# A table of places in place of the list scheduler, in a fused attention and MLP kernel

## The chip, the cores and the metric

The kernel runs on one core of a Trainium2 chip. A core has a matrix engine (TensorE, PE in the profile), two engines for elementwise work (VectorE, DVE, and ScalarE, ACT), a general one (GpSimd, POOL), and SyncE (SP), which here only issues transfers. Each engine executes its own list of instructions strictly in order; between engines, and between an engine and a transfer, semaphores make one wait for another. Transfers (DMA) are issued by SP, ScalarE and POOL from their own queues and run on 16 shared DMA engines. The metric is the device time of one execution in microseconds (us).

## The reference: what is computed

Attention with a window of 128 positions and 4 sink keys over 4 batches, 8 heads, 768 positions of 64 numbers each; the heads laid side by side give x with 768 rows of 512 per batch. Then a LayerNorm, a two-layer MLP (512 to 2048 to 512), and x added to its result.

```python
keep = (pos_k < 4) | ((rel >= 0) & (rel < 128))
a = softmax(where(keep, q @ k.T / 8, -1e9))
x = concat_heads(a @ v)
xn = (x - mean(x)) / sqrt(var(x) + 1e-6) * g_ln
out = x + maximum(xn @ w_ch1, 0) @ w_ch2
```

## The kernel before

**Tiles and chunks.** The 3072 rows are 24 tiles of 128 rows (tile t, six per batch) and 12 chunks of two tiles (chunk c has tiles 2c and 2c+1). For a chunk, q and k are loaded and transposed (`chunk`, L605), v is loaded (`load_v`, L585), the scores are multiplied out, exponentiated on ScalarE and masked (`attend_tile` L724 for chunks 0 and 1, `attend` L777 for the others), and `value` (L844) multiplies with v, divides by the row sums, takes the LayerNorm's mean and variance, centres the tile (L885) and transposes it into xnt. Then `halves` (L927) or `mlp` (L1006) form the first MLP layer and `wino` (L1074), for all chunks but the first two, the second with seven products p1 to p7 (L1109) of matrix sums s1 to s4 (L1092); the products are added up to the result by VectorE (tm at L1123, o at L1130), and stored by SP (L1070, L1154, L1159).

**How data arrives.** The first chunk's q and k come in as f32 halves by SP and ScalarE (L620), are cast to bf16 (L637) and transposed on TensorE. Chunks 1 to 3 come by POOL and are transposed on TensorE too (n4b in the trace is one such load, transposed at L672). From chunk 4 on q and k are loaded by POOL into buffers nat (L687) and transposed by SP's transposing transfers (L569, kq<-nat). The transposes of the centred tiles are PE transposes for the first two chunks and SP transfers (L569, xnt<-xc) from chunk 2 on. The first four rows of v (the sink keys) for the batches 1 to 3 come in sixteen small SP loads (L535, 3 KB each) into one buffer vc, out of which the tables vs1 (VectorE, L539), vs2 and vs3 (POOL) are made; the table vs0 of batch 0 is made at L707.

**What sets the order.** None of this is emitted directly. 1137 calls of `P.op` record a step each: a name, the engines that can do it with a modelled cost, a priority, a function that emits it, and the buffers that it reads and writes. Buffers belong to rings of a fixed number of slots. `Plan.run` (L115) is a list scheduler: it goes forward in a modelled time, and gives each step an engine, a start and a slot in each of its rings, by priorities and modelled costs of work and transfers. The steps are then sorted by start, and one loop emits them; since each engine executes in that order, the sort decides what stands behind what on every engine and in every queue of transfers. Before the loop, up to 24 us of the plan, idle places of TensorE are filled with products on a tile named junk (L1236), whose results nobody reads.

```python
    order = P.run()
    items = [(o.start, o.seq, o) for o in order]
...
    items.sort(key=lambda z: (z[0], z[1]))
...
            if s < 0:
                nc.tensor.matmul(o[:, 0:-s], lhsT=junk[:, 0:128], rhs=junk[:, 0:-s], start=True, stop=True)
            else:
                o.emit(o.eng)
```

Of the kernel before, what the change touches and what calls it, by code (L numbers as in the profile page):

```python
# [13 lines left out]
class Buf:  # L14


    def __init__(self, name, ring=None):
        self.name, self.ring = name, ring
        self.writers, self.users = [], []
        self.slot = None  # L20
        self.left = 0
# [43 lines left out]
class Plan:  # L65


    SEM = 0.035
    TO_PE = 0.11
    PE_DRAIN = 0.18  # L70
    SWITCH = 0.095
    LANES = 8
    SHARED = 36.0
    MIXED = 1e9
    DMA_BUSY = {}

    def __init__(self):
        self.ops = []
        self.rings = {}
# [25 lines left out]
        self.ops.append(o)  # L105
        return o

    def lat(self, src, dst):
        if src.eng == "PE" and src.dma is None:
            return -self.PE_DRAIN if dst == "PE" else self.SEM  # L110
        return self.TO_PE if dst == "PE" else self.SEM

    WINDOW = {"PE": 0.2, "ACT": 0.25, "DVE": 0.25, "POOL": 0.25, "SP": 0.0}

    def run(self):  # L115
        free = {"PE": 0.9, "ACT": 0.75, "DVE": 0.9, "POOL": 1.5, "SP": 0.75}
        lanes = {"POOL": [0.0] * self.LANES, "HW": [0.0] * self.LANES}
        n_dma = {"POOL": 0, "HW": 0}
        dma_free = {"POOL": 0.0, "HW": 0.0, "all": 0.0}
        mode = "n"  # L120
        ready = [o for o in self.ops if o.n_wait == 0]
        order = []
        tensor = sorted((o for o in self.ops if "PE" in o.engs), key=lambda o: (o.prio, o.seq))
        while ready:
            while tensor and tensor[0].start is not None:
                tensor.pop(0)
            head = tensor[0] if tensor else None
            cand = {}
            first = min([o.prio for o in ready for b in o.bufs if b.ring == "pair" and b.slot is None], default=1e9)
            for o in ready:  # L130
                if "PE" in o.engs and o is not head and o.prio >= PAR["strict"]:
                    continue
                need = [b for b in o.bufs if b.ring and b.slot is None]
                ok, avail, took = True, 0.0, {}
                for b in need:
                    used = [u for s in took.values() for u in s.units]
                    ss = [s for s in self.rings[b.ring] if not s.held and not any(u in used for u in s.units)
                          and not (s.lent and o.prio > first)]
                    if not ss:
                        ok = False  # L140
                        break
                    since = max([min(s.free_at for s in ss)] + [min(free[e] for e in o.engs) - 0.3])
                    s = min((s for s in ss if s.free_at <= since), key=lambda s: (s.rank, s.free_at))
                    took[b] = s
                    avail = max(avail, s.free_at)
                if not ok:
                    continue
                best = None
                for e, (occ, lat) in o.engs.items():
                    r = max([free[e], o.nb, avail + (self.TO_PE if e == "PE" else self.SEM)]  # L150
                            + [d.end + self.lat(d, e) for d in o.deps])
                    if e == "PE" and o.mode_in != mode:
                        r = max(r, free[e] + self.SWITCH)
                    if o.dma is not None:
                        q = "POOL" if e == "POOL" else "HW"
                        r = max(r, lanes[q][n_dma[q] % self.LANES])
                    if best is None or r + lat < best[0] - 1e-9:
                        best = (r + lat, e, r)
                cand.setdefault(best[1], []).append((best[2], o, took))
            if not cand:  # L160
                stuck = sorted(ready, key=lambda o: o.prio)[:8]
                raise RuntimeError("plan stuck: " + ", ".join(
                    f"{o.name}[{','.join(b.name for b in o.bufs if b.ring and b.slot is None)}]" for o in stuck))
            e = min(cand, key=lambda e: min(c[0] for c in cand[e]))
            t0 = min(c[0] for c in cand[e])
            st, o, took = min((c for c in cand[e] if c[0] <= t0 + self.WINDOW[e]), key=lambda c: (c[1].prio, c[1].seq))
            for b, s in took.items():
                b.slot = s
                s.take()
            o.eng, o.start = e, st  # L170
            occ, lat = o.engs[e]
            free[e] = st + occ
            if e == "PE":
                mode = o.mode_out
            if o.dma is None:
                o.end = st + lat
            else:
                busy, first, last = o.dma
                q = "POOL" if e == "POOL" else "HW"
                if st < self.MIXED:  # L180
                    at = max(st + occ + first, dma_free[q], dma_free["all"] if st < self.SHARED else 0.0) + busy
                    dma_free[q] = dma_free["all"] = at
                    o.end = at + last
                else:
                    real = self.DMA_BUSY.get(o.dma, busy)
                    other = dma_free["HW" if q == "POOL" else "POOL"] > st + occ + first
                    at = max(st + occ + first, dma_free["all"]) + real
                    dma_free[q] = dma_free["all"] = at
                    o.end = at + last + max(0.0, busy - real) + (PAR["mix"][q == "POOL"] if other else 0.0)
                lanes[q][n_dma[q] % self.LANES] = o.end  # L190
                n_dma[q] += 1
            for b in o.bufs:
                b.left -= 1
                if b.left == 0 and b.ring:
                    b.slot.give(min(u.start for u in b.users), max(u.end for u in b.users))
            ready.remove(o)
            order.append(o)
            for s in o.succ:
                s.n_wait -= 1
                if s.n_wait == 0:  # L200
                    ready.append(s)
        assert len(order) == len(self.ops), "cycle in the plan"
        order.sort(key=lambda o: (o.start, o.seq))
        return order


def pe(us):
    return {"PE": (us, us + Plan.PE_DRAIN)}


def act(n):
# [13 lines left out]
SW = (0.9, 0.7, 0.9)  # L225
# [4 lines left out]
HW_X = (1.0, -0.2, 0.6)  # L230
SW_2 = (0.65, 0.7, 0.9)
HW_T = (0.10, 0.8, 0.8)

Plan.DMA_BUSY = {SW: 1.03, HW_X: 0.55}

LOW, HIGH = 1e-9, 1e9
NEG = -1e30
NEVER = -1e9

PAR = dict(split=(3, 4, 5, 6, 7), gsum=-8.0, guard=183.0, strict=40.0, win=0.4, tr=-8.0, sc=-5.3, sc1=-2.0, av=2.0, trx=9.0, by_dma=4, x_by_dma=2, g_on_w=2, av2=20.0, avi=1.0, behind=5, gtt=9.0, ramp=0.3, vs0=2.6, vpb=12.0,  # L240
           w1p=(0.15, 1.7, 2.05, 2.8), pm=2, w2p=(4.5, 4.51, 4.52, 4.53), by_tile=2, wino=2, vp=(0.0, 0.1, 2.0, 2.1, 4.2, 4.3), ld1=0.05,
# [3 lines left out]
def general(tc, nc, slots, pairs, ones, ident_f, ident, w1, w2, mhalf, g_s, g_r, q, k, v, out, scale):  # L245
# [23 lines left out]
    with tc.For_i(0, B, 1) as b:  # L269
# [5 lines left out]
        for r in range(RB):  # L275
# [23 lines left out]
            for i, t in enumerate(sc):  # L299
# [74 lines left out]
def kernel(  # L374
# [141 lines left out]
    def picks(e):  # L516
        V.memset(pick, 0.0)
        for a in range(2):
# [761 lines left out]
```

## Time and profile before

| what | us |
| --- | --- |
| three runs | 208.88, 208.98, 209.49 |
| median of the runs | 208.98 |
| span of the profiled execution, from first to last instruction | 206.6 |
| TensorE busy | 199.4 (97%) |
| VectorE busy | 179.6 (87%) |
| ScalarE busy | 119.7 (58%) |
| GpSimd busy | 118.7 (57%) |

One execution was profiled; the profile's own time is its span, and the runs measure a little more than the span, for what lies around the first and last instruction. The granted TensorE clock was 1.000 throughout. A line of the trace reads: start in us, duration in us, engine, line of the kernel, operation, what it writes and from what, and a count where neighbours of one kind are drawn together; in brackets stands how long the engine idled before it and what ended that. SPq, POOLq and ACTq are transfers in the queues of these engines; their duration is that of the issue, not of the transfer. A line of a source view has the shortest, median and longest duration in ns, and the first and last start in us. PEld is the loading of weights into TensorE, which runs beside its products.

### The profile page before, as it was taken

What the parts mean: (1) busy time and instruction counts of PE and PEld (TensorE: products, weight loads), DVE (VectorE), ACT (ScalarE), POOL (GpSimd) and SP (SyncE); (2) the same over time, 40 slices, a digit from 0 to 9 for tenths busy, and PEclk for the clock granted to TensorE, in tenths of its full rate; (3) what the DMA queues carried; (4) which work ended last, traced back from release to release, by engine and by line L of the source; (5) the groups of instructions that cost most, each with busy time, mean ns of one, the idle gap of its engine ahead of it and who ended that gap; (6) DMA issues with size and microseconds to landing.
All of it is one profiled execution on the core that took longest, in us unless ns stands there. A gap on an engine that the chain in (4) does not pass through costs nothing.

```text
span 206.6 us, 6790 instructions
## 1 busy us (share of the span) xinstructions
PE 199.4 (97%) x2766; PEld 165.6 (80%) x2766; DVE 179.6 (87%) x437; ACT 119.7 (58%) x187; POOL 118.7 (57%) x170
## 2 busy tenths in 40 slices
PE   6888999999999999999999999999999999999994
PEld 2557996674698897898998988988988988988993
DVE  7589769899599899899989989989989989998693
ACT  3649477839555655666486486485486585560620
POOL 7977475279039029959649949968627229125000
PEclk9999999999999999999999999999999999999999
DMA  5999999999999999999999999899976411210302
GB/s 117 146 195 195 197 181 205 199 158 171 186 200 124 124 191 101 121 174 101 175 152 137 113 159 143 109 171 114 194 117 101 128 33 23 106 32 19 108 27 84
DMA packets 101341, 27.55 MB, mean 133 GB/s; under 512 B 89652, under 2 KB 99128, under 8 KB 101304
## 3 DMA queue, kind: packets, MB, share of 16 engines
q0 software_dynamic: 67712, 13.37, 81.7%
q1 hardware_dynamic: 33304, 13.43, 34.1%
q8 instruction: 22, 0.36, 0.7%
q10 hardware_dynamic: 288, 0.26, 0.4%
q14 instruction: 15, 0.12, 0.2%
HBM read 27.31 MB, written 6.29 MB: 163 GB/s over the span
## 4 chain that ended last, share of the span: by engine, by line
PE 90%; DMA 3%; DVE 3%; POOL 2%; issue 0%; DVEq 0%
PE one L1109 31%; PE one L1027 20%; PE one L958 12%; PE one L1058 7%; PE one L1020 7%; PE pair L854 5%; PE pair L802 4%; DMA n4b<-in_q_dram 3%; PE one L672 1%; PE pair L721 1%; POOL nat L626 1%; PE one L714 1%; DVE xnt L907 1%; DVE kq L595 1%; POOL vn L589 0%; DVE st L874 0%
## 5 line engine op out<-in xcount | busy, mean ns | idle before, releaser
L1027 PE MATMUL one<-xnt,w 128*128 128x256 bf16 x384 | 46.8, 273 | 0.0
L814 ACT ACTIVATE pe<-pair 128x1024 bf16<-128x1024 f32 (+1 forms) x40 | 36.3, 963 | 18.2 <-PE pair L802 18.2
L1037 ACT ACTIVATE hq<-one 128x512 bf16<-128x512 f32 x58 | 33.4, 590 | 17.9 <-PE one L1020 9.4
L1027 PEld LDWEIGHTS <-w 128*128 128x128 bf16 x384 | 36.3, 98 | 4.0
L1109 PEld LDWEIGHTS <-hs 128*128 128x128 bf16 x320 | 31.0, 98 | 4.0
L882 POOL TENSOR_SCALAR st<-st 128x1 f32<-128x1 f32 x24 | 6.4, 266 | 44.4 <-DVE rec L868 27.5
L826 DVE TENSOR_TENSOR pe<-pe,mask 128x1024 bf16<-128x1024 bf16 (+1 forms) x35 | 27.1, 799 | 1.6 <-ACT pe L814 1.4
L969 ACT COPY tz<-one 128x512 f32<-128x512 f32 x24 | 13.9, 585 | 20.6 <-PE one L958 19.2
L1109 PEld LDWEIGHTS <-hq 128*128 128x128 bf16 x240 | 22.2, 98 | 4.1 <-issue 0.5
L589 POOL DMA_DIRECT2D vn<-in_v_dram x24 | 21.9, 922 | 2.2 <-DMA w<-in_moe_w_ch_dram 1.2
L983 ACT ACTIVATE hq<-hq 128x512 bf16<-128x512 bf16 x24 | 15.1, 630 | 13.1 <-DVE hq L980 12.6
L1109 PE MATMUL one<-w,hq 128*128 128x256 bf16 x160 | 19.2, 273 | 0.0
L980 DVE TENSOR_TENSOR hq<-one,tz 128x512 bf16<-128x512 f32 x24 | 16.4, 684 | 1.9 <-PE one L958 1.0
L1130 DVE TENSOR_TENSOR ot<-one,tm 128x256 f32<-128x256 f32 x40 | 15.9, 412 | 2.1 <-PE one L1109 1.8
L1123 DVE TENSOR_TENSOR tm<-one,x 128x256 f32<-128x256 f32 x40 | 16.6, 414 | 1.2 <-PE one L1109 1.1
L870 DVE TENSOR_TENSOR x<-pair,rec 128x512 bf16<-128x512 f32 x24 | 16.6, 691 | 0.8
L874 DVE BATCH_NORM_STATS2 st<-x 128x6 f32<-128x512 bf16 x24 | 16.5, 687 | 0.2
L1020 PE MATMUL one<-xnt,w 128*128 128x128 bf16 x256 | 16.0, 219 | 0.5 <-DVE xnt L907 0.5
L687 POOL DMA_DIRECT2D nat<-in_q_dram x16 | 14.2, 893 | 3.7 <-DMA w<-in_moe_w_ch_dram 3.7
L938 POOL TENSOR_TENSOR xt<-xnt 128x256 bf16<-128x256 bf16 x16 | 12.2, 778 | 7.1 <-DMA xnt<-xc 7.0
L687 POOL DMA_DIRECT2D nat<-in_k_dram x16 | 14.8, 928 | 2.4 <-DMA w<-in_moe_w_ch_dram 2.4
L1020 PEld LDWEIGHTS <-w 128*128 128x128 bf16 x256 | 14.6, 98 | 1.6 <-issue 0.8
(130 smaller groups left out, 387.7 us busy)
## 6 DMA issues: line engine op xcount, KB each, us to landing
out_dram<-ot SPq DMA_DIRECT2D x17, 256.0 KB
w<-in_moe_w_ch_dram POOLq DMA_DIRECT2D x8, 512.0 KB, 12.8
vn<-in_v_dram POOLq DMA_DIRECT2D x24, 128.0 KB, 6.9
nat<-in_k_dram POOLq DMA_DIRECT2D x17, 128.0 KB, 4.6
nat<-in_q_dram POOLq DMA_DIRECT2D x17, 128.0 KB, 4.9
out_dram<-ot SPq DMA_DIRECT2D x14, 128.0 KB
kq<-nat SPq DMA_TRANSPOSE x32
xnt<-xc SPq DMA_TRANSPOSE x20
```

The costliest lines, as they stand in the source:

```text
L589: loads[b * RB + r, "v"] = P.op(f"vld{t}", {"POOL": (0.87, 0.9)}, prio, lambda e: G.dma_start(bv.t[:, :, 0:64], v[b, :, 128 * r:128 * (r + ...
L687: lambda e, nat=nat, ap=ap: G.dma_start(nat.t, ap), writes=[nat], dma=SW if c < 6 else (*SW[:2], PAR["llag"]), after=behind(c, 0 if soon e ...
L814: P.op(f"ex{c}{hp}", {"ACT": act(2 * n)}, d + 0.1 + 0.05 * j, lambda e, pp=pp, pb=pb: nc.scalar.activation(pb.t[:, :, 0:n], pp.t[:, :, 0:n ...
L826: V.tensor_mul(pb.t[:, :, 0:n], pb.t[:, :, 0:n], mm),
L870: P.op(f"x{t}", {"DVE": dve(512)}, d + xo + 0.11, lambda e: V.tensor_tensor(x.t.rearrange("p (a h c) -> p a h c", a=2, c=64), pv()[:, :, : ...
L874: P.op(f"bn{t}", {"DVE": fix(0.60)}, d + xo + 0.12, lambda e: V.bn_stats(st.t[:, 8:14], x.t), reads=[x], writes=[st, mv])
L958: nc.tensor.matmul(b.t[:, 128 * h:128 * h + 128], lhsT=lt[:, kk, 128 * h:128 * h + 128], rhs=rh[:, kk, :], start=first and h == 0 and kk = ...
L1020: nc.tensor.matmul(ph.t[:, 128 * s:128 * s + 128], lhsT=w1[u // 2][:, j, 128 * s:128 * s + 128], rhs=xnt.t[:, j, 128 * (u % 2):128 * (u % ...
L1027: nc.tensor.matmul(ph.t[:, 256 * s:256 * s + 256], lhsT=w1[ht // 4][:, j, 128 * (ht % 4):128 * (ht % 4 + 1)], rhs=xnt.t[:, j, :], start=j ...
L1037: nc.scalar.activation(hg.t[:, u % 4, :], ph.t, AF.Relu)
L1109: nc.tensor.matmul(at(r), lhsT=get(left, g)[:, v, s, :], rhs=rhs, start=first and n == 0, stop=n == 7, skip_group_check=True)
L1123: return P.op(f"tm{name}_{c}", {"DVE": dve(256, 1.14)}, pr - PAR["kp"], lambda e: V.tensor_tensor(tm[name].t, at(r), xs[i].t[:, sl], op=AL ...
```

## The change

`Plan.run` no longer schedules. Two literals give its answer: SCHEDULE has, for each of the 1137 steps in the order in which they were recorded, a letter for the engine (P, A, V, G, S) and a place in hundredths; SLOTS has a digit for each ring buffer, its slot. The scheduler's model (latencies, windows, costs of transfers, `lat`) goes away. What the steps compute, their dependences, the sort and the loop that emits them are as before; 19 lines fewer stand ahead of the kernel's body, so that L1109 becomes L1090.

```diff
-    SEM = 0.035
-    TO_PE = 0.11
...
     def run(self):
-        free = {"PE": 0.9, "ACT": 0.75, "DVE": 0.9, "POOL": 1.5, "SP": 0.75}
-        lanes = {"POOL": [0.0] * self.LANES, "HW": [0.0] * self.LANES}
...
-            st, o, took = min((c for c in cand[e] if c[0] <= t0 + self.WINDOW[e]), key=lambda c: (c[1].prio, c[1].seq))
...
-        order.sort(key=lambda o: (o.start, o.seq))
-        return order
+        engines = dict(P="PE", A="ACT", V="DVE", G="POOL", S="SP")
+        table = SCHEDULE.split()
+        assert len(table) == len(self.ops)
+        for o, entry in zip(self.ops, table):
+            o.eng, o.start = engines[entry[0]], int(entry[1:]) / 100
+            o.end = o.start + o.engs[o.eng][1]
+        for b, n in zip(dict.fromkeys(b for o in self.ops for b in o.bufs if b.ring), "".join(SLOTS.split())):
+            b.slot = self.rings[b.ring][int(n, 36)]
+            for u in b.slot.units:
+                u.lives.append((min(o.start for o in b.users), max(o.end for o in b.users)))
+        return sorted(self.ops, key=lambda o: (o.start, o.seq))
...
+SCHEDULE = """
...
+SLOTS = """
```

The order that results differs as follows.

- TensorE: the same 288 steps and the same 75 changes between kinds of product; the first 29 steps in the same order; 24 fillers instead of 25. Behind that, neighbours change places: chunk 3's first W1 products (L1027) stand ahead of chunk 2's last three W2 products p4, p5 and p3.
- Engine: twelve steps go from ScalarE to VectorE (evacuations, relus, scalings of W1), nine from VectorE to ScalarE, among them the second cast of the first chunk (L637).
- ScalarE: the activation that brings in the table of Exp (L481) stood first and now stands behind chunk 4's work.
- VectorE: vs0 (L707) moves ahead of the second tile's centring and of the copy with gain (L907) into xnt; vs1 (L539) moves from chunk 2 to a place right ahead of chunk 2's result additions (L1130).
- SP: the sixteen loads of v's sink rows stood one after another at the head. Now the order is: g, two loads of the first chunk, the transpose of tile 5, then the sixteen loads in between the transposes of tiles 4, 6 and of chunk 4's q and k and two stores, with the last of the sixteen right ahead of tile 7's transpose.
- SP's last four stores: first the half that is computed last but one, then the other three. Before, two of them stood ahead of it.
- POOL: the loads of later chunks are issued later, closer to their use.

More of the change, by code (lines that the diff above doesn't have):

```diff
@@ L65 @@
 class Plan:
-    SEM = 0.035
-    TO_PE = 0.11
[L70 to L75, printed above, removed]
     def __init__(self):
@@ L106, in op @@
         return o
[L108 to L113, printed above, removed]
-    def run(self):
-        free = {"PE": 0.9, "ACT": 0.75, "DVE": 0.9, "POOL": 1.5, "SP": 0.75}
-        lanes = {"POOL": [0.0] * self.LANES, "HW": [0.0] * self.LANES}
[L118 to L165, printed above, removed]
-            st, o, took = min((c for c in cand[e] if c[0] <= t0 + self.WINDOW[e]), key=lambda c: (c[1].prio, c[1].seq))
[L167 to L202, printed above, removed]
-        order.sort(key=lambda o: (o.start, o.seq))
-        return order
@@ L207, in pe @@
+PE_DRAIN = 0.18
 def pe(us):
-    return {"PE": (us, us + Plan.PE_DRAIN)}
+    return {"PE": (us, us + PE_DRAIN)}
 def act(n):
@@ L232 @@
 HW_T = (0.10, 0.8, 0.8)
-Plan.DMA_BUSY = {SW: 1.03, HW_X: 0.55}
 LOW, HIGH = 1e-9, 1e9
@@ new lines @@
+V1202 P1181 A1248 G777 G939 P1308 V1533 P1340 A1391 V1615 P1481 A1532 V1742 P1379 A1483 P1858 P1879 V1949 V1973 V2045
+V2118 G2209 V2305 P2355 V2398 P1511 A1624 V1801 P1670 A1765 V1871 P2024 P2045 V2127 V2151 V2223 V2296 G4004 V2458
+P2552 V2633 G1176 G1248 P2671 A2738 P2717 A2830 G1869 G2122 P2956 A3145 V3704 A3053 V3159 A3036 P3381 A3534 V3644
+A3443 V3548 P3785 P3854 V3935 V3959 V4069 V4194 G4216 V4369 S4851 P3806 V3924 V4236 V4309 V4395 G4416 V4568 S4606
+G2892 G2644 P4303 A4417 P4257 A4325 V5066 G3576 G3824 P4541 A4600 V4763 A4670 V4846 P4770 A4899 V4984 A4829 V4926
@@ new lines @@
+P5124 V5197 V5221 V5294 V5393 G5415 V5738 S5816 P5076 V5561 V5585 V5678 V5764 G5785 V5983 S6022 G3482 S4971 G4088
+S5516 G3389 S5091 G3917 S5366 G3141 G2505 P6028 A6139 V6545 A6230 V6452 A6564 P6368 A6581 V6701 A6472 V6641 P6774
+P6843 V6973 V6997 V7117 V7190 G7211 V7316 S7362 P6795 V6902 V7057 V7235 V7307 G7329 V7420 S7482 G6216 S6779 G4508
+S6899 G5868 S6427 G6042 S6557 G6390 G5498 P7599 A7787 G7893 A7678 V7890 A7770 P8026 A8176 V8408 A8085 V8341 P8390
+P8500 V8570 V8617 V8689 V8814 G8836 V9058 S9103 P8593 V8677 V8904 V8976 V9049 G9070 V9312 S9357 G7412 S8325 G6303
@@ new lines @@
+S8085 G7673 S8205 G6129 S8664 V9901 G6477 G5955 P9221 A9279 V9550 A9350 V9434 P9452 A9510 V9693 A9581 V9780 P9938
+V9984 V10008 V10169 V10321 G10342 V10458 S10504 P9962 V10309 V10333 V10491 V10564 G10585 V10706 S10751 G8356 S9752
+G7586 S9872 G8657 S9512 G8197 S9632 G7499 G8110 P10592 A10799 G11016 A10707 V11013 A11082 P10932 A10990 V11211 A11099
+V11286 P11251 P11452 V11658 V11682 V11871 V11943 G12035 V12127 S12226 P11404 V11509 V11533 V11742 V11931 G11952 V12044
+S12106 G10755 S11350 G9872 S11230 G9785 S11110 G10190 S10990 G10103 G10668 P12126 A12315 G12421 A12223 V12818 A12206
@@ new lines @@
+V16721 G16742 V17045 S17090 P16072 V16230 V16254 V16444 V16516 G16538 V16653 S16698 G13725 S15763 G14888 S15608 G14975
+S16073 G15145 S15953 G13812 G16621 P16657 A16736 G16842 A16828 V17284 A17147 P16997 A17055 V17188 A17164 V17344 P17315
+P17469 V17538 V17562 V17699 V17819 G17840 V18139 S18373 P17517 V17622 V17759 V17831 V17956 G17978 V18172 S18218 V3854
+V4892 V4694 V6301 V3315 V4627 V4661 V5354 V3393 V4203 V5527 V6009 V4019 V4594 V5890 V5645 P1550 A1716 P1762 A2085
+P1927 A2036 P2093 A2425 P2180 A2289 P2267 A2376 P2377 A2486 P2465 V2573 P3198 P3428 P3902 P3988 V4129 S4786 P3514
@@ new lines @@
+P4075 P4161 P4359 V4467 S5301 P2574 V2693 P2860 V2968 P2772 V2881 P3285 A3393 P3024 V3219 P3111 A3237 P3688 A3809
+P3601 A3858 P4588 P4674 P4817 P4903 V5096 S6677 P4445 P4990 P5148 P5235 V5402 S7019 V5161 V3888 A5031 A3748 A4970
+V4532 V4727 V3608 V5030 A3626 V3279 A3687 A5654 V4810 A3907 A5092 P5408 A5517 P5321 V5467 P5496 A5604 P5583 A5715
+P5670 V5923 P5932 A6040 P5757 A5866 P5844 A6090 V6109 V6076 V6043 V6153 V6232 V6199 V6797 V6512 P6096 V6265 P6271
+V6380 P6184 V6416 P6415 V6605 P6590 V6761 P6677 V6866 V6830 P6891 V7199 S8784 S8819 P6502 A6673 P7066 A7175 P6979
@@ new lines @@
+A7088 P7153 A7262 P7415 A7524 P7328 A7436 P7240 A7349 P7502 V7611 V7349 V7704 V7671 V7811 V7737 V7857 V8099 V8022
+P7666 V7775 P7754 V7950 P7841 V7986 P7929 V8063 P8073 V8198 P8160 V8269 V8305 P8292 V8581 S9992 S8629 S9477 V5800
+V6913 V8138 V7453 G8038 G8443 G8284 G8585 P8248 A8314 P8455 A8522 P8411 V8477 A8892 P8548 A8614 P8641 V8749 A8843
+P8773 V8839 A8991 P9079 A9150 P8904 A9040 P8817 A8942 P8685 A8794 P8992 A9100 V9243 V9103 V9345 V9164 V9391 V9209
+V9643 V9481 P9124 V9276 P9267 V9829 P9355 V9514 P9498 V9608 P9586 V9744 P9674 V9865 V9931 P9806 V10068 S11505 S10624
@@ new lines @@
+A19117 P19165 V19247 A19324 P19210 V19312 A19389 P19429 A19500 P19254 V19377 P19078 V19187 P18946 V19055 P19342 A19450
+V19593 V19449 V19626 V19514 V19695 V19559 V19794 V19899 P19474 V19659 P19561 V19827 P19649 V19758 P19749 V19863 P19836
+V19945 P19924 V20069 V20033 P20011 V20120 S20152 S20187 S20117 S20222 V18049 P18357 V18511 P20176
+"""
+SLOTS = """
+0001000123001000000301112011130112230130410122211150603331022145102781109010444255503311601012103416603077120345121005
+6210071088209936170134102890101210aa41bb522435056103410051c0020d116307101100671101210e223f3320345231038921003100540445
```

35 lines of the change are left out of this document (added).

## The prediction

> **What bounds the kernel now.** I read the page's first lines first, then the chain of waits, then the busy time by stage.
>
> ```profile
> span 206.6 us, 6790 instructions
> PE 199.4 (97%) x2766; PEld 165.6 (80%) x2766; DVE 179.6 (87%) x437; ACT 119.7 (58%) x187; POOL 118.7 (57%) x170
> PE 90%; DMA 3%; DVE 3%; POOL 2%; issue 0%; DVEq 0%
> ```
>
> TensorE is busy for 97% of the span and holds 90% of the chain that ended last. DVE is the next fullest with 87%, and it is second in nothing that the chain shows. What matters is therefore where TensorE idles at all. The next lines are stages in us: length, busy time of each engine with its count, then granted clock (1.00), DMA share, GB/s.
>
> ```profile
> 13.00:20.00 7.00, 6.27 (x135) 5.03 (x130) 6.45 (x12) 5.84 (x9) 5.26 (x9) 1.00 1.41 199
> 20.00:45.00 25.00, 24.98 (x420) 19.58 (x419) 20.80 (x48) 15.16 (x23) 14.01 (x20) 1.00 1.71 189
> 45.00:60.00 15.00, 15.00 (x158) 9.80 (x154) 12.69 (x32) 10.12 (x16) 7.13 (x11) 1.00 2.08 179
> 60.00:75.00 15.00, 15.00 (x208) 12.74 (x206) 13.55 (x33) 8.28 (x13) 6.94 (x10) 1.00 1.60 145
> 150.00:180.00 30.00, 30.00 (x463) 26.43 (x462) 28.12 (x64) 19.19 (x32) 12.15 (x19) 1.00 0.34 85
> 180.00:203.50 23.50, 23.41 (x252) 20.62 (x249) 19.79 (x50) 8.58 (x16) 4.86 (x8) 1.00 0.16 48
> ```
>
> From 20 us on nothing is idle but 0.02 + 0.09. So 0.73 (13 to 20 us) + 0.11 is all that a better order can win in these rows; a little more hides inside "busy", where a product waits for an operand but its record is drawn long. In the last W2 group the starts tell it:
>
> ```profile
> 185.67 1.05 PE L1109 MATMUL one<-n4a,hs 128*128 128x256 bf16 x8
> 186.67 1.03 PE L1109 MATMUL one<-n4c,hs 128*128 128x256 bf16 x8
> 187.67 0.60 PE L1109 MATMUL one<-w2t,hq 128*128 128x256 bf16 x4
> 67.79 1.05 PE L1109 MATMUL one<-n4b,hs 128*128 128x256 bf16 x8
> 68.67 1.04 PE L1109 MATMUL one<-w,hs 128*128 128x256 bf16 x8
> 69.55 1.91 PE L1027 MATMUL one<-xnt,w 128*128 128x256 bf16 x16
> ```
>
> Eight products that are fed go by in 0.88 (67.79 to 68.67); at 185.67 and 186.67 a step takes 1.00, so 0.25 is lost there. With some 0.2 for others of that kind, the gain can be at most 0.73 + 0.11 + 0.25 + 0.2 = 1.3 us. A loss has no such limit, so the question is which of the moved steps comes too late for TensorE.
>
> **The change part by part.** The 1137 steps, what each depends on and what it computes stay. The order on each engine, the engine of 21 steps and the buffer of each result change. TensorE has the same 288 steps with the same 75 changes of kind, the first 29 in the same order, so its own work costs the same.
>
> *The ramp.* ScalarE's table load (L481) moves from its first place to far behind, so the load now happens before the first thing that ScalarE computes, the cast at L637, whose queue place is behind its waits for the raw loads. The second cast, done by VectorE before, follows on ScalarE.
>
> ```profile
> 1.95 1.28 ACT L481 ACT_TABLE_LOAD   x1 [1.95 <-PEq L1261]
> 5.04 0.62 ACT L637 CAST hq<-n4a 128x512 bf16<-128x512 f32 x1 [1.59 <-DMA n4a<-in_q_dram]
> 12.17 1.02 ACT L758 ACTIVATE pe<-pair 128x1024 bf16<-128x1024 f32 x1 [1.98 <-PE pair L754]
> 12.73 1.08 PE L672 MATMUL one<-ident,n4b 128*64 128x128 bf16 x32 [0.60 <-DMA n4b<-in_q_dram]
> 13.41 1.23 DVE L595 COPY kq<-one 128x1024 bf16<-128x1024 bf16 x1 [0.42 <-PE one L672]
> 18.01 0.69 DVE L907 TENSOR_TENSOR xnt<-one,gt 128x512 bf16<-128x512 bf16 x1
> 18.75 1.05 PE L1020 MATMUL one<-xnt,w 128*128 128x128 bf16 x16 [0.45 <-DVE xnt L907]
> 19.21 0.42 DVE L707 TENSOR_TENSOR vs<-one,sel 128x260 bf16<-128x260 f32 x1
> q0 software_dynamic: 4398, 1.09, 161.1%
> q1 hardware_dynamic: 182, 0.04, 4.3%
> ```
>
> The attention of the first tile is pushed back by about 1.28 + 0.5 (the second cast's wait), taken as 1.6 to 1.8. It has cover: TensorE waited 0.60 for n4b and ScalarE idled 1.98 before its first activation of the second tile; I take 1.3 as hidden and 0.3 as left. The path that releases the solid part is VectorE's run from 13.41 to 18.70; it starts with n4b, which the casts don't touch. Into this run goes L707 with 0.42, behind it before: some 0.3 more. Together +0.6. At the most nothing covers: 1.7 + 0.3 = +2.0. At the least all of it is covered and the small loads of V that leave this stretch hasten n4b: in 5.5 to 12.6 us they are 4.3 beside 161.1, 2.6% of 7.1 us, −0.2.
>
> The Trainium skill ("ScalarE: Activation LUTs", section "What ACT_TABLE_LOAD costs") puts the load at about 1283 ns and adds some 1380 ns of drain on a switch. The row agrees with the first, 1.28 us; the drain isn't seen here, since nothing ran ahead of this load. By the page, an estimate, the sum would be 1.4 us higher.
>
> *The middle.* Sixteen small loads of V (L535) stood at the head of SP's queue; now they stand between the transposes of chunks 2 to 5. Between tile 5's transpose and tile 7's, SP issues seven transposes, all sixteen small loads and two stores. A queue executes in order.
>
> ```profile
> L569 SPq DMA_TRANSPOSE kq<-nat x32: 1190/1220/2368, 53.2 to 159.5; - x32
> L535 SPq DMA_DIRECT2D vc<-in_v_dram x16: 250/298/309, 3.6 to 11.4; - x16
> 57.25 0.53 SPq L1070 DMA_DIRECT2D out_dram<-ot  x1
> 57.88 2.37 SPq L569 DMA_TRANSPOSE kq<-nat  x1
> 62.79 1.19 SPq L569 DMA_TRANSPOSE xnt<-xc  x1
> 94.41 2.00 SPq L569 DMA_TRANSPOSE xnt<-xc  x1
> 100.34 1.29 POOL L938 TENSOR_TENSOR xt<-xnt 128x256 bf16<-128x256 bf16 x2 [1.64 <-DMA xnt<-xc]
> 184.55 1.19 SPq L569 DMA_TRANSPOSE xnt<-xc  x1
> 187.13 1.48 POOL L938 TENSOR_TENSOR xt<-xnt 128x256 bf16<-128x256 bf16 x2 [3.06 <-DMA xnt<-xc]
> 46.24 0.41 DVE L885 TENSOR_SCALAR xc<-x,st 128x512 bf16<-128x512 bf16 x1
> 64.35 0.41 DVE L1130 TENSOR_TENSOR ot<-one,tm 128x256 f32<-128x256 f32 x1
> ```
>
> A transpose holds SP 1.22 us, a store 0.53, a small load 0.30 of its own and (11.4 − 3.6)/15 = 0.52 from start to start: I take 0.40. That is 8.5 + 6.4 + 1.1 = 16.0 us (14.4 with 0.30, 17.6 with 0.5). A transpose right behind a store took 2.37, 1.15 more: one such gives 17.1, which I take, two with the upper price 19.8. The start is the end of tile 5's centring, 46.65, with two 0.4 us VectorE steps now ahead of it and the ramp's 0.6: 48.0. So tile 7's transpose (62.79 before) is issued at 65.1, between 62.4 and 67.8. From issue to use I find 2.6 us (184.55 to 187.13) and 5.9 (94.41 to 100.34); between them 4.25: landed at 69.35. Chunk 3's products (69.55 before) are due earlier, since three W2 groups of 0.87 now come behind them: 69.55 + 0.6 − 2.6 = 67.5. TensorE waits 1.9 us. The ends are 0 (issue by 62.4 and 2.6 of transit) and 67.8 + 5.9 − 67.5 = 6.2.
>
> The vs sums (L539) need all sixteen small loads and stand in VectorE's queue right ahead of the W2 additions that begin at 64.35 (L1130); behind them wait more additions, the masks, and in turn the banks into which TensorE writes. With VectorE at 13.55 of 15.00, a wait here isn't made up soon. I take none of it above the 1.9, because both end with the same run of SP.
>
> *The last groups.* The sums that the products at 185.67 and 186.67 take stand two places earlier on VectorE: −0.25, from 0 to −0.5 with the other small losses.
>
> ```profile
> 202.91 0.96 DVE L1130 TENSOR_TENSOR ot<-one,tm 128x256 f32<-128x256 f32 x2
> 203.35 0.88 SPq L1154 DMA_DIRECT2D out_dram<-ot  x2
> 97.80 0.34 SPq L1154 DMA_DIRECT2D out_dram<-ot  x1
> ```
>
> *The tail.* Before, two of the four last stores went out ahead, and the last was issued at 203.35 + 0.88 − 0.34 = 203.9 (a store of this line holds SP 0.34). Now the store that needs the last addition but one (ready at 203.36) stands first, and three follow at about 0.37 each (0.34 and a gap of 0.03): 204.5. That is +0.6; 1.1 if four stores that leave together also land later by half a step each, 0.5 at the least.
>
> *Costed at nothing.* The large POOL loads come later in POOL's order and nearer to their use. They land ahead of need by the plan's order; what hides them is that a load of 128 KB takes 4.9 us to land, and its transpose sits in an SP queue which is late anyway; without that cover scores of chunks 4 to 5 wait as long as SP does. Twelve steps go to VectorE and nine to ScalarE, so VectorE has three more, at the 0.4 to 0.7 us of its rows above some 2 us in 206.6, spread over stages that have 1.45 to 2.31 free of 15; if all of it fell where VectorE is full, the 2 us would count.
>
> ```profile
> nat<-in_q_dram POOLq DMA_DIRECT2D x17, 128.0 KB, 4.9
> ```
>
> *The sum.* 206.6 + 0.6 + 1.9 − 0.25 + 0.6 = 209.45 us of span. The median of the runs, 208.98, lies 2.38 above the span of the profiled execution; what lies around it is the same: 211.8 us.
>
> **The rivals.**
>
> *SP keeps up.* The queue takes its 14.4 us, transit is 2.6, and the middle costs nothing. For it: the small loads take 0.30, and the transposes rarely wait. Against it: SP starts late, and a store stands in the list. Point: landing of tile 7 before 67.5. Then 211.8 − 1.9 = 209.9.
>
> *VectorE is held as well.* The last small load is issued just ahead of tile 7's transpose, about 64.6, and lands 2.6 to 5.9 later, 67.2 to 70.5, where the additions are due at 65.0: 2.2 to 5.5 us, in which TensorE runs out of banks. The middle, 3.85, is 1.9 more than the forecast's wait: 213.7.
>
> *Faster.* The queue is hidden, the tail's later issue is hidden under the landing of the others, the ramp's idle time and the small steps are won: 208.98 − 1.3 = 207.7, up to 208.3 if half comes. For it: only 0.84 of idle is visible at all, and the small loads leave the busiest stretch of DMA. Against it: the new waits above. Point: the first large W1 group starts before 18.75 and the middle shows no wait.
>
> *No effect.* TensorE is full, so order on the others is hidden both ways: 209.0.
>
> **How the numbers follow.** Forecast 211.8 (from 210.4 to 213.3) 0.43; VectorE held as well 0.12; SP keeps up 0.13; no effect 0.13; faster 0.19. Changes under 0.3%, 0.63 us, can't be told from none, so "same" is 208.35 to 209.6. Faster 0.19, same 0.13, slower 0.68. The range goes from 208.0, which leaves out half of "faster", to 214.2, which leaves out half of "VectorE held": 0.16 outside.
>
> **What would show it.** Ramp: a table load near 4.5 to 6 us and the W1 products that began at 18.75 begin near 19.35. Middle: TensorE idle before chunk 3's first 128x256 products by about 1.9 us, released by the DMA of xnt; the vs sum of L539 after 60 us with a wait for the DMA of vc. Tail: the last store issued about 1.1 us after the last addition began its second half, not 0.5. I am wrong if TensorE shows no idle between 60 and 75 us, or if the first large products start before 18.75.

## The result, and the profile after

The changed kernel takes 223.19 us (median of 4 runs, 222.50 to 225.16) against 209.18 us before: 1.069 times as long (95% interval 1.064 to 1.075). The forecast was 211.8 us, with a range that ended at 214.2. The direction and the two costly places (the middle and the tail) were right; the sizes were not. A few executions take over 1.5% longer than the fastest of the same kernel, and they are left out where they would decide a comparison.

The profiled execution has a span of 221.0 us, 14.4 more than before. The page's first lines and the stages of it (us: length, busy time of TensorE, weight loads, VectorE, ScalarE, GpSimd, then granted clock, DMA share, GB/s):

```profile
span 221.0 us, 6744 instructions
PE 203.1 (92%) x2765; PEld 165.7 (75%) x2765; DVE 178.5 (81%) x440; ACT 117.1 (53%) x184; POOL 115.6 (52%) x170
...
45.00:60.00 15.00, 14.63 (x145) 9.19 (x146) 13.31 (x36) 8.56 (x13) 4.21 (x8) 1.00 1.09 103
60.00:75.00 15.00, 8.93 (x121) 6.98 (x120) 8.55 (x24) 6.33 (x11) 8.56 (x10) 0.95 1.70 140
75.00:90.00 15.00, 15.00 (x180) 12.59 (x179) 11.71 (x29) 6.30 (x10) 5.94 (x9) 0.94 0.78 108
90.00:105.00 15.00, 14.47 (x204) 12.25 (x202) 14.44 (x31) 8.63 (x15) 10.43 (x15) 1.00 1.25 133
105.00:120.00 15.00, 14.37 (x202) 12.33 (x200) 14.17 (x33) 8.26 (x16) 8.36 (x13) 1.00 1.10 115
```

VectorE does no more than before (178.5 against 179.6 us). TensorE lost 6.07 us of 15 between 60 and 75, where it had been full, and its clock was granted at 0.95 from 60 to 75 us and at 0.94 from 75 to 90. The instructions of that place, from the trace of the changed kernel (start, duration, and in brackets the idle time before it):

```profile
64.97 1.19 SPq L550 DMA_TRANSPOSE xnt<-xc  x1
66.20 0.82 SPq L516 DMA_DIRECT2D vc<-in_v_dram  x2
67.12 1.32 SPq L550 DMA_TRANSPOSE xnt<-xc  x1
...
67.72 1.05 PE L1090 MATMUL one<-n4c,hs 128*128 128x256 bf16 x8
...
72.10 0.43 DVE L520 TENSOR_TENSOR vs<-vc,sel 128x260 bf16<-128x260 f32 x1 [5.73 <-DMA vc<-in_v_dram]
...
74.28 1.87 PE L1008 MATMUL one<-xnt,w 128*128 128x256 bf16 x8 [5.51 <-DMA xnt<-xc]
75.94 1.52 PE L1090 MATMUL one<-w2t,hq 128*128 128x256 bf16 x8
77.30 1.04 PE L1090 MATMUL one<-n4b,hs 128*128 128x256 bf16 x8
```

Tile 7's transpose was issued by SP at 67.12; TensorE stood still for 5.51 us until it had landed, and VectorE for 5.73 us until the last small load of V had. The eight products at 74.28 then took until 75.94, 1.66 us where before 0.87 was enough, the next eight 1.36. Short windows over the same place show the clock at that time (columns as above):

```profile
70.00:74.00 4.00, 0.00 (x0) 0.00 (x0) 1.90 (x5) 0.00 (x0) 0.00 (x0) 0.94 2.09 162
74.00:76.00 2.00, 1.72 (x9) 1.26 (x10) 2.00 (x5) 0.00 (x0) 0.00 (x0) 0.50 1.65 172
76.00:78.00 2.00, 2.00 (x16) 1.63 (x15) 0.77 (x3) 0.60 (x1) 0.00 (x0) 0.77 1.23 254
78.00:80.00 2.00, 2.00 (x45) 1.62 (x43) 1.83 (x6) 0.00 (x0) 0.00 (x0) 1.00 0.30 116
```

After the pause the granted clock was 0.50, and 1.00 again only by 78 us. The Trainium skill says why in "TensorE: Matmul & The Clock Gate", section "What's actually happening": after about 3.4 us of idling the clock is gated to half, and it takes as long of work to free it. The trace agrees with the order of size only: if the clock is either whole or half, the shares above put it at half from about 73.5 to 76.9 us (an estimate), that is from 4.7 us into the pause until 2.6 us of work were done.

At the end of the trace of the changed kernel:

```profile
213.72 0.49 PE L1090 MATMUL one<-w,hs 128*128 128x256 bf16 x3
...
214.26 0.96 DVE L1111 TENSOR_TENSOR ot<-one,tm 128x256 f32<-128x256 f32 x2
214.70 1.80 SPq L1135 DMA_DIRECT2D out_dram<-ot  x4
```

TensorE's last group of eight starts 11.35 us later than before (202.37 to 213.72); the other 3.05 us of the 14.4 come behind it. Four stores now leave together from 214.70; the last is issued about 216.1 (214.70 + 1.80 less the 0.4 that an issue takes), and the end comes 4.9 us after that, where before it came 2.7 after (203.9 to 206.6).

The start of the same TensorE step in both traces divides the rest. Before, the second tile's W1 products start at 18.75, and chunk 5's scores and the last group so:

```profile
77.92 0.25 PE L802 MATMUL pair<-kq,kq 64*64 64x64 bf16 x4
202.37 1.04 PE L1109 MATMUL one<-w,hs 128*128 128x256 bf16 x8
```

In the changed kernel the first two are:

```profile
19.00 1.05 PE L1001 MATMUL one<-xnt,w 128*128 128x128 bf16 x16
86.55 0.25 PE L783 MATMUL pair<-kq,kq 64*64 64x64 bf16 x4
```

The W1 products are 0.25 later. Chunk 5's scores are 8.63 later, so 8.4 of it arise between: the wait of 5.51, 1.3 for the half clock, and 1.6 of smaller losses (one is a wait of 0.55 for a transpose of chunk 4's q and k). The last group is 11.35 later, so 2.7 more arise after chunk 5's scores, among others in the stages from 90 to 120 us above, where TensorE is 0.53 and 0.63 short.

### The profile page after: what moved, and what is told of

The parts are those of the page before. It is cut to its first block, busy times and chain, and to the rows that moved or that the text cites. A ratio compares the mean times of both kernels' runs of the same rounds, so it can differ in the third digit from the quotient of the medians.

```text
span 221.0 us, 6744 instructions
## 1 busy us (share of the span) xinstructions
PE 203.1 (92%) x2765; PEld 165.7 (75%) x2765; DVE 178.5 (81%) x440; ACT 117.1 (53%) x184; POOL 115.6 (52%) x170
## 5 line engine op out<-in xcount | busy, mean ns | idle before, releaser
L1008 PEld LDWEIGHTS <-w 128*128 128x128 bf16 x384 | 37.0, 99 | 10.1 <-issue 5.8
L1018 ACT ACTIVATE hq<-one 128x512 bf16<-128x512 f32 x53 | 30.7, 595 | 26.3 <-PE one L1008 16.5
L795 ACT ACTIVATE pe<-pair 128x1024 bf16<-128x1024 f32 (+1 forms) x40 | 36.9, 963 | 12.5 <-PE pair L783 12.5
L1090 PEld LDWEIGHTS <-hs 128*128 128x128 bf16 x320 | 30.2, 98 | 6.0 <-issue 1.7
L807 DVE TENSOR_TENSOR pe<-pe,mask 128x1024 bf16<-128x1024 bf16 (+1 forms) x35 | 24.3, 711 | 2.5 <-ACT pe L795 2.4
L1090 PEld LDWEIGHTS <-hq 128*128 128x128 bf16 x240 | 22.9, 99 | 3.9 <-issue 0.3
L1090 PE MATMUL one<-w,hq 128*128 128x256 bf16 x160 | 19.7, 273 | 0.0
L1073 DVE TENSOR_TENSOR hs<-hq 128x512 bf16<-128x512 bf16 x40 | 15.4, 419 | 2.4 <-ACT hq L1018 2.2
L939 PEld LDWEIGHTS <-hq 128*128 128x128 bf16 x256 | 15.7, 98 | 0.9 <-issue 0.3
L668 POOL DMA_DIRECT2D nat<-in_q_dram x16 | 14.7, 923 | 1.8 <-DMA w<-in_moe_w_ch_dram 1.6
```

Of the source, the lines that this page charges most:

```text
L795: P.op(f"ex{c}{hp}", {"ACT": act(2 * n)}, d + 0.1 + 0.05 * j, lambda e, pp=pp, pb=pb: nc.scalar.activation(pb.t[:, :, 0:n], pp.t[:, :, 0:n ...
L807: V.tensor_mul(pb.t[:, :, 0:n], pb.t[:, :, 0:n], mm),
L939: nc.tensor.matmul(b.t[:, 128 * h:128 * h + 128], lhsT=lt[:, kk, 128 * h:128 * h + 128], rhs=rh[:, kk, :], start=first and h == 0 and kk = ...
L1008: nc.tensor.matmul(ph.t[:, 256 * s:256 * s + 256], lhsT=w1[ht // 4][:, j, 128 * (ht % 4):128 * (ht % 4 + 1)], rhs=xnt.t[:, j, :], start=j ...
L1018: nc.scalar.activation(hg.t[:, u % 4, :], ph.t, AF.Relu)
L1090: nc.tensor.matmul(at(r), lhsT=get(left, g)[:, v, s, :], rhs=rhs, start=first and n == 0, stop=n == 7, skip_group_check=True)
```

## The experiments

S is the theory that the sixteen small loads in SP's queue are the cause; P, that GpSimd's later loads are, by crowding the transfers. In what is expected, theories of one experiment are marked by a letter too (V, D, W, O, X). Where the edit is in the changed kernel, a dictionary of names gives steps another place in the table:

```diff
-            o.eng, o.start = engines[entry[0]], int(entry[1:]) / 100
+            o.eng, o.start = engines[entry[0]], MOVED.get(o.name, int(entry[1:]) / 100)
```

**The small loads back at the head of SP's queue.**

```diff
+MOVED = {f"vcd{i // 4}{i % 4}": 30 + 0.3 * i for i in range(16)}
```

> The changed kernel, but the sixteen small loads of V go back to the head of SP's queue. Theory S (they delay tile 7's transpose and vs1): SP had no gap from 48.8 to 67.1 us, and sixteen loads at 0.30 to 0.47 are 6 us of it, so tile 7's transpose is issued near 61, TensorE's wait of 5.5 us and the slower clock after it (1.1 us) go, and so do VectorE's wait of 5.7 and what came of it later (2.6 us of lag between 90 and 126 us): 223.2 - 9.2 = 214, or 216.6 if the later lag stays. Rival P (POOL issues its loads for chunks 4 and 5 between 62 and 69 us, and they make the transpose's transfer take 7.0 us): the wait stays at 3 us or more, 220 or above.

216.06 us (1.035 of before, 1.027 to 1.042; the changed kernel 1.069). The stage of this run that had the pause, the issue of both chunk 3 transposes, chunk 5's scores and the last group:

```profile
60.00:75.00 15.00, 15.00 (x208) 12.75 (x206) 14.11 (x36) 7.58 (x13) 8.93 (x12) 1.00 1.78 150
```

```profile
59.69 3.12 SPq L550 DMA_TRANSPOSE xnt<-xc  x2
67.14 1.04 PE L1008 MATMUL one<-xnt,w 128*128 128x256 bf16 x8
...
78.14 0.25 PE L783 MATMUL pair<-kq,kq 64*64 64x64 bf16 x4
...
205.31 1.04 PE L1090 MATMUL one<-w,hs 128*128 128x256 bf16 x8
```

TensorE has no gap and a clock of 1.00; chunk 3's products start at 67.14. S holds, P alone does not: GpSimd issues the same eight loads here, about 1 us earlier (61.06 to 68.22). By the medians 7.1 us came back. In the trace all of the middle's 8.4 did: chunk 5's scores are 0.22 later than before. The profiled execution is the fastest of the five (214.40 us); the other four took 215.86 to 216.52 at granted clocks of 0.991 to 0.996, and what they lost is not known. From chunk 5's scores to the last group 127.17 us pass, as in the changed kernel (before 124.45), so the later lag of 2.7 us is not what VectorE's wait leaves behind.

**vs1 six steps later on VectorE, the small loads still between.** `MOVED = dict(vs1=67.3)`

> The changed kernel, but VectorE makes vs1 six steps later, behind the first additions and the masks of chunk 4; the small loads stay between the transposes. Theory S with the transpose as what ends last: TensorE's wait for xnt stays at about 5.5 us, and only what VectorE lost comes back, up to 2.6 us: 220.6 to 223. Rival V (VectorE's wait at vs1 holds up TensorE): the wait shrinks to 2 us or less, 217 to 219.

222.31 us (1.062, 1.054 to 1.071). VectorE's wait is down to 0.93 us, TensorE's is 5.18 (lines of this run):

```profile
71.40 0.43 DVE L520 TENSOR_TENSOR vs<-vc,sel 128x260 bf16<-128x260 f32 x1 [0.93 <-DMA vc<-in_v_dram]
73.24 1.86 PE L1008 MATMUL one<-xnt,w 128*128 128x256 bf16 x8 [5.18 <-DMA xnt<-xc]
```

In the changed kernel it is the transpose that ends last, not VectorE; the difference of 0.9 us between the medians is within the noise. (In the next run, which changes nothing in the middle, the profile puts TensorE's wait of 5.89 us down to a mask of VectorE, L807. In the changed kernel the same product began 0.46 us before that mask had ended, so it doesn't need the mask.)

**The last four stores in the order of before, alone and with the small loads.** `MOVED = dict(st220=200.9, st232=201.0)`; in the second run both sets of places.

> The changed kernel, but the last four stores in the order of before (two of them ahead of the one that needs the last addition but one). If the four stores that leave together are what the tail lost (from TensorE's last product to the end 5.7 us, before 2.7): 223.2 - 3.1 = 220.1. If it is the later issue alone, as the prediction had it: 223.2 - 0.6 = 222.6.

> The changed kernel with both: the small loads at the head and the stores in the order of before. The two are far apart in time, so the gains should add: 214 - 3.1 = 210.9 by theory S, 217 by rival P.

220.79 us (1.055, 1.047 to 1.064) and 212.05 us (1.016, 1.008 to 1.023). By the medians the stores are worth 2.4 us alone and 4.0 beside the small loads. The traces agree on 3.1 in both: from TensorE's last group to the end 4.2 us pass with the old order of the stores (215.30 to 219.5 and 205.67 to 209.9) and 7.3 with the new one. Together the two moves give back 11.1 of the 14.0 us.

**The same two moves alone, in the kernel before.** The scheduler's own places, with a few replaced after it has run:

```diff
-        assert len(order) == len(self.ops), "cycle in the plan"
+        for o in order: o.start = MOVED.get(o.name, o.start)
...
+MOVED = dict(vcd12=48.04, vcd10=48.05, vcd21=50.4, vcd32=53.0, vcd30=53.01, vcd02=53.02, vcd22=54.4, vcd31=57.0, vcd33=57.01, vcd13=57.02, vcd00=57.03, vcd23=57.04, vcd01=57.05, vcd11=57.06, vcd03=58.0, vcd20=58.01, vs1=61.87)
```

> The kernel before, list scheduler and all, but the sixteen small loads of V stand between SP's transposes as in the changed kernel, and vs1 ahead of chunk 2's first result addition. Theory S (these loads alone hold up tile 7's transpose): about 13 of them at 0.45 us come after SP's one long gap, tile 7's transpose is issued near 68 in place of 62.8, TensorE waits 3 to 5.5 us before chunk 3's products: 209 + 3 to 6.5, so 212 to 215.5. Rival P (late POOL loads are needed too, and this kernel's are early): under 1 us, 209 to 210.

219.41 us (1.046, 1.039 to 1.054): more than expected. Lines and stages of this run (the line without a time is of the view of transfers: the time from issue to landing of tile 6's transpose, issued at 65.33):

```profile
xnt<-xc SPq DMA_TRANSPOSE x1, 6.4
68.25 1.19 SPq L569 DMA_TRANSPOSE xnt<-xc  x1
72.45 0.43 DVE L539 TENSOR_TENSOR vs<-vc,sel 128x260 bf16<-128x260 f32 x1 [7.91 <-DMA vc<-in_v_dram]
74.53 1.86 PE L1109 MATMUL one<-w2t,hq 128*128 128x256 bf16 x8 [7.91 <-DVE tm L1123]
```

```profile
60.00:75.00 15.00, 7.09 (x89) 5.82 (x87) 6.59 (x18) 4.25 (x7) 6.50 (x8) 0.82 1.41 141
75.00:90.00 15.00, 15.00 (x187) 11.86 (x186) 11.50 (x28) 7.42 (x11) 3.22 (x6) 0.84 0.17 50
```

The move is enough by itself. Here, with TensorE's old order, VectorE ends last: TensorE waits 7.91 us for an addition queued behind vs1, and works at 0.82 and 0.84 of its clock around that. If the clock is either whole or half, it was at half from about 69.6 to 79.8 us (an estimate from the two shares), 5.3 us of it work, which costs some 2.6 us.

Rival P doesn't get its test here, though: GpSimd's loads are not early in the kernel before either. These are its six of that time:

```profile
62.27 1.87 POOL L687 DMA_DIRECT2D nat<-in_k_dram  x2
64.12 1.78 POOL L687 DMA_DIRECT2D nat<-in_q_dram  x2
65.86 1.79 POOL L589 DMA_DIRECT2D vn<-in_v_dram  x2
```

They leave from 62.27 to 67.65 us (in this run 0.1 later), where the changed kernel issues eight from 62.07 to 69.2. Before, tile 7's transpose was issued at 62.79, when only the first of them had left; in this run tile 6's, at 65.33, comes among them, and it took 6.4 us to land.

For the stores, `MOVED = dict(st220=200.7, st232=200.8)`:

> The kernel before, but of its last four stores the one that needs the last addition but one stands first in SP's queue. If four stores that leave together land late (the run with the stores put back gained 2.4 us): 209 + 2 to 3 = 211 to 212. If only the issue is later, as the prediction had it: 209.6.

211.84 us (1.013, 1.009 to 1.018), span 209.8 us. The stores that leave together cost this kernel 3 us, not 0.6; from its last group to the end 7.3 us pass (202.49 to 209.8).

**Five of GpSimd's late loads later still.** `MOVED = dict(kld61=73.4, qld61=73.5, vld10=73.6, vld13=73.7, vld12=73.8)`

> The changed kernel, with five of the eight loads that POOL issues between 62 and 69 us put behind tile 9's statistics, so that they leave after 84 us. If those loads are why tile 7's transpose took 7.0 us from issue to landing, it lands in about 4.5 and TensorE's wait falls from 5.5 to 3: 220 to 221, if nothing later waits for the five loads. If the transpose is slow for what SP itself issues, the 7.0 and the 5.5 stay: 223 or above.

219.63 and 220.74 us in the two of its four runs that can be compared, near the expected 220 to 221 and below all runs of the changed kernel (222.50 or more); two runs are too few for an interval. The trace, of the run at 220.74, shows the part in question:

```profile
67.10 2.20 SPq L550 DMA_TRANSPOSE xnt<-xc  x1
70.54 0.10 PEld L1008 LDWEIGHTS <-w 128*128 128x128 bf16 x1 [1.14 <-DMA xnt<-xc]
71.12 1.03 PE L1008 MATMUL one<-xnt,w 128*128 128x256 bf16 x8 [1.43 <-DVE ot L1111]
```

Issued at the same 67.1, the transpose is in use 3.4 us later and not 7.2. What TensorE then still waits for is VectorE's addition behind vs1 (ot): in the changed kernel this addition ended at 72.87, so without the late transpose TensorE would have stood there until about 72.9 in place of 74.28 (an estimate). GpSimd's queue between 64 and 74 us (packets, MB, and the time of its packets as a share of the 16 engines' time, which can pass 100%), in the changed kernel and then in this run:

```profile
q0 software_dynamic: 7437, 0.94, 160.1%
```

```profile
q0 software_dynamic: 2909, 0.37, 57.5%
```

So loads that are in flight beside it lengthen the transfer. Chunk 5's scores start at 82.56, 4.0 us earlier than in the changed kernel; then TensorE waits 1.38 us (93.72) and 1.49 us (102.01), the second for a transpose of q and k, and at the last group (211.78) 1.9 of the 4.0 are left.

**ScalarE's table load back at the start**, on top of the run at 212.05 us: `tab0=1.75, tab=1.81`.

> The changed kernel with the small loads at the head and the stores in the old order (212.05 us), and ScalarE's table load back at its first place. In the run without this the load stood at 4.97 us ahead of the first cast, the first tile was 1.6 us behind, and at TensorE's wait for n4b all of it but 0.06 was gone. So by the reading that the wait for n4b covers it: 211.8 to 212.3, the first products of the second tile still near 12.8. By the prediction's +0.3: 211.7.

212.24 us (1.014, 1.006 to 1.022). Where the load stands is not to be seen in the time. TensorE's transposes of n4b start at 12.72 us with the load at the start and at 12.80 without, the second tile's W1 products at 18.87 and 18.89.

**The last 3.3 us.** The run at 212.05 us has a span of 209.9, 3.3 more than before. All of these start from it. First, single VectorE steps (`wsum2=82.9, o4_2=96.91, o4_0=96.92, kts2=99.35, mk71=110.95`), since TensorE's waits there have lines like these of that run:

```profile
84.54 1.15 DVE L904 TENSOR_TENSOR hq<-w,w 128x1024 bf16<-128x1024 bf16 x1
...
85.61 0.74 DVE L1111 TENSOR_TENSOR ot<-one,tm 128x256 f32<-128x256 f32 x2
86.08 1.03 PE L1090 MATMUL one<-w,hs 128*128 128x256 bf16 x8 [0.40 <-DVE ot L1111]
```

> The changed kernel with the small loads at the head and the stores in the old order (212.05 us), and in addition VectorE's additions for chunks 3 to 5 ahead of longer steps (wsum2, two masks, kts2) that stood before them. Theory D (the rest of the loss, about 3.3 us, is TensorE waiting some 0.2 to 0.6 us at a time for a bank that an addition has not freed): five of these waits, 2.0 us together, shrink to 0.5: 210 to 210.7. Rival (VectorE is as full in either order, a wait only moves): 211.7 to 212.3.

211.93 us: nothing. The waits moved: in this run TensorE stands 0.9 us for a mask. Then ten steps back on ScalarE, alone and with these moves:

```diff
-            o.eng, o.start = engines[entry[0]], MOVED.get(o.name, int(entry[1:]) / 100)
+            o.eng, o.start = "ACT" if o.name in ON_ACT else engines[entry[0]], MOVED.get(o.name, int(entry[1:]) / 100)
+ON_ACT = "rl0_7 rl1_0 rl1_1 rl2_1 rl2_4 rl3_7 w1g13 w1g20 w1g22 w1g31".split()
```

> As the run at 212.05 us (small loads at the head, stores in the old order), with the ten relus and scalings of W1 after 20 us that the table moved to VectorE put back on ScalarE at the same places. Theory W (VectorE has 5.1 us of these more and 2.4 us of others less, is 2.3 us behind when chunk 5's scores are multiplied, and TensorE pays in small waits): VectorE comes level, the waits between 85 and 120 us shrink from 2.9 to 1 or less: 209.7 to 210.5. Rival (the order alone, whichever engine): 211.5 to 212.3.

> The same with the additions ahead of wsum2, two masks and kts2 as well. Theory W: with VectorE no longer behind, the order of these steps can count or not, 209.3 to 210.3. Rival: as without it, 211.5 or more. A version of the changed kernel that is faster than the kernel before (208.7) would show here.

212.05 and 212.14 us: nothing either, though VectorE's busy time falls from 178.5 to 173.8. Then VectorE's list in the order of before (130 and 308 places are given anew), and TensorE's with it:

> As the run at 212.05 us (small loads at the head, stores in the old order); VectorE's 150 steps between the places 60 and 128 stand in the order that they had before, every other engine's order is the changed one. Theory O (the last 3.3 us lie in the order of VectorE's list, in many places of it, so that five moves and five microseconds of relief could only shift the waits): the waits between 85 and 120 us go, 2.9 of them, and 209 to 210 us are left. Theory X (the orders of the engines fit each other: VectorE's old order beside the others' new one is no better): 211.5 or more.

> The same, with all of VectorE's steps from place 26 on in the order of before. Theory O: 208.5 to 209.7, since the waits of 20 to 45 us and at 163 us (1.1 together) go too. Theory X: 211.5 or more.

> As the run at 212.05 us, with VectorE's and TensorE's steps from place 60 on in the order of before; ScalarE, GpSimd and SP keep the changed one. Theory O: as the first, 208.5 to 210. Theory X with VectorE and TensorE as the pair that has to fit: 208.5 to 210 here alone, and 211.5 or more in the other two. If GpSimd's late loads and sums hold the rest: 211 or more here as well.

219.29, 237.69 and 221.47 us (medians of the runs that can be compared), all slower. TensorE's longest waits in the second of them (total, times, longest):

```profile
PE one L1090 <- DVE hs L1073: 7.5, 4, 4.0
PE pair L835 <- DVE pe L807: 5.6, 9, 1.2
```

Theory O falls: the old order of one engine, or of two, beside the new order of the others is much worse than either whole. Last, two more steps by hand, wsum2 into a gap (`wsum2=77.5`) and kts2 behind an addition (`kts2=100.7`):

> The changed kernel with the small loads at the head, the stores in the old order, ten relus and scalings back on ScalarE and the five moves (212.14 us), and two more from its trace: wsum2 goes into a gap of 1.15 us in which VectorE waited for the first W2 product of chunk 3, and kts2 behind chunk 4's last addition. If the rest is many small misfits that can be taken out one at a time, 0.9 and 0.6 us of TensorE's waits go: 210.7. If a wait only moves to the next step on the list, 211.7 to 212.3. No version from the table is then expected under 208.9.

211.42 us (1.015, 1.009 to 1.020), the same as 212.14 within its interval. No version made from the table came under the kernel before.

## Why the prediction was right or wrong, point by point

**What bounds.** Right. TensorE had no idle time to give, and the losses that were traced are stretches in which a moved step came too late for it. "At most 1.3 us to win, no limit on a loss" stands.

**Which step failed.** Most of the 11.4 us between the forecast and the result lies in the middle: +1.9 in the sum, +8.4 measured. The wait was 5.51 and not 1.9, and the half clock behind it (1.3) was no term. The next two are the last groups and the orders (−0.25 in the sum, +2.7 measured) and the tail (+0.6 in the sum, +3.05 measured).

**The ramp, +0.6.** The mechanism was right, the size too large: +0.25. The table load did come ahead of the cast (at 5.24 us), and the wait for n4b covered all of it but 0.02 (18.87 and 18.89 with the load at the start and without), where I had left 0.3.

**The middle, +1.9.** The right queue, the right transpose, the right steps; the wait was 5.51. Three numbers of the sum were off. The list was issued from 48.8 to 67.1, 18.3 us in place of 17.1 and 0.8 later: +2.0. The issues by themselves took 17.2, as priced; the other 1.1 are the gaps between them, for which the sum has no term. From issue to use the transpose took 7.2 us, where I had taken the middle between rows of 2.6 and 5.9: +2.9. That row of 5.9 was no upper bound: at 65 to 67 us the transpose comes among GpSimd's loads. In the kernel before they leave from 62.27 to 67.65, so the trace of before already had them at the time that I forecast for the issue, 65.1. That the products were due at 68.77 and not 67.5 took 1.3 off again. The wait lay inside my bounds of 0 to 6.2; a third of the way up was the wrong choice.

**What the pause costs besides, not in the sum.** The half clock: 1.66 + 1.36 in place of 0.87 + 0.88 for two groups, 1.3 us. No row of before shows a pause of that length, and a forecast of 1.9 us gave no reason to look for it; the upper end of 6.2 did.

**VectorE held as well.** It was a rival at +1.9 us. VectorE did wait 5.73 us. Taking that wait away left 5.18 us of TensorE's, because the transpose ends last; with the transpose early (the run with five loads later) VectorE ended last, and so it did in the kernel before with the small loads moved. Two waits at one place do not add up, and here the smaller one stands only some 1.4 us behind the larger.

**The last groups, −0.25.** The mechanism came, the gain did not. The group that starts at 183.90 before, and the same group after:

```profile
183.90 1.91 PE L1109 MATMUL one<-w,hq 128*128 128x256 bf16 x16
```

```profile
195.46 1.91 PE L1090 MATMUL one<-w,hq 128*128 128x256 bf16 x16
197.42 1.05 PE L1090 MATMUL one<-n4a,hs 128*128 128x256 bf16 x8
198.31 1.04 PE L1090 MATMUL one<-n4c,hs 128*128 128x256 bf16 x8
199.18 1.04 PE L1090 MATMUL one<-w2t,hq 128*128 128x256 bf16 x8
```

The two steps of 1.00 took 0.89 and 0.87, 0.24 won; the one ahead of them took 1.96 in place of 1.77, 0.19 lost. The allowance for other small losses had the wrong sign: from chunk 5's scores to TensorE's last group 2.7 us were lost. The trace names 1.5 of them as waits of 0.2 to 0.4 us, all but one for additions of VectorE that read a bank before TensorE may write it again.

**The tail, +0.6.** Right step, wrong term: I priced the later issue (203.9 to 204.5 by the prediction's sum) and left the landing of four stores at 0.5 at the most. The issue is 0.9 later against TensorE's last group (216.1 − 213.72 = 2.4, before 203.9 − 202.37 = 1.5), and the landing 2.2 later (4.9 in place of 2.7): 3.05.

**Costed at nothing.** GpSimd's loads: as a term of their own nothing shows them; the loads in flight lengthen the transposes that the small loads push among them. With five of them moved away the transpose took 3.4 us and not 7.2, but in the kernel before, with its own six loads, one took 6.4, so the table's later places for the loads are not needed for it. The engine swaps: right as far as tried, ten of the 21 undone change nothing. The orders of TensorE and VectorE: some 3 us that I had left out. What in them it is stays open; five moved steps, two more, ten swaps and the old order on one or two engines did not find it. Shown is only that none of the steps moved held it alone, and that the old order on one or two engines did not mix with the new one on the others.

## What to carry to other kernels

A table that only reorders can cost 7% without adding an instruction: price each queue in which something is moved ahead, by what it issues and by what else will be in flight at that moment, and take the transit from the busiest such place, not from the middle of two rows. The trace of before shows what is in flight at the new place of a moved transfer. A wait of TensorE that may reach 4 or 5 us can have its price in clock too (1.3 and some 2.6 us here). A suspected move is best tried twice, undone in the new kernel and alone in the old one; here the two gave 7.1 and 10.7 us, and in the old kernel another wait ended last.

## What the runs showed of the hardware

A pause of 5.51 us halved the granted clock for about 3.4 us, 2.6 of them work, and one of 7.91 us for about 10 us, 5.3 of them work (estimates from the shares above). One of 1.43 us (five loads later) did not: the clock stayed at 1.00 in every 2 us window around it. The same small transpose took 3.4 us from issue to use with 57.5% of GpSimd's queue time beside it and 7.2 with 160.1%. Four stores of 128 KB that left within 1.8 us ended the execution 4.9 us after the last issue; with two of them sent ahead it was 2.7.
